# Queries and keys as scaled fp16 pairs that stay on chip, and an FFN in eight blocks

## The chip, the cores and the metric

The kernel runs on one core of one Trainium2 chip. The metric is device microseconds from start to end of one execution. The engines are named as in the profile: PE (TensorE, matmuls), PEld (its weight loads), DVE (VectorE), ACT (ScalarE), POOL (GpSimd), SP (SyncE, which here only issues DMAs). Each engine works through its own instructions strictly in the order in which they were written to it.

## The reference

Clustered attention, then a maxout FFN. There are 4 batches, 8 heads, 768 positions and a head size of 64; queries, keys and 16 centroids per head are normed, each query and key belongs to the centroid with the largest product, and a query sees only keys of its own cluster.

```python
mask = q_assign[:, :, :, None] == k_assign[:, :, None, :]
scores = scale * np.matmul(q, k.transpose(0, 1, 3, 2))
scores = np.where(mask, scores, -1000000000.0)
attn = softmax(scores)
attn_out = np.matmul(attn, v)                     # (4, 8, 768, 64) -> x (3072, 512)
h = np.maximum(np.maximum(x @ w1, x @ w2), x @ w3)  # (3072, 768)
out = h @ w_out                                   # (3072, 512)
```

Inputs and output are fp32.

## The kernel before

To keep fp32's accuracy, every operand of a matmul is held as a pair of a rounded part and the rest, and each product is summed from two or three matmuls. q and k of one head stand in one tile of 128 partitions: q^T in the upper 64, k^T in the lower 64. The tile `qk` of a pair of heads holds four versions of both heads (`AQ, BQ, BK, AK`, two heads, 768 columns), made from the loaded `stage` tile: `qk_prep` casts the high part to fp32r (ACT) and subtracts it for the low part (POOL, once DVE), and `qk_moves` copies parts between the upper and the lower 64 partitions, by DMA from batch 1 on, by ACT and POOL in batch 0. Two matmuls per half row then give the whole score: one of 128 rows (`aq` with `ak`), one of `K2` = 80 rows (`bq` with `bk`), whose last 16 rows carry the one-hot cluster of the query and that of the key, shifted by `BIG`, so that a pair of different clusters gets a large negative score. `cluster_scores` multiplies the pair with the centroids, `cluster_rows` finds the winner by two block transposes and compares on DVE, and writes the one-hot rows into the qk tile.

One **step** is one head and 128 queries (`scores`): four score matmuls into a `big` tile of PSUM (three buffers), a scaled negation with row minimum on DVE (line 489), the exponential on ACT (line 492), the reciprocal of the sum on DVE, and the split of the probabilities into two fp16 halves `hl`, by ACT and DVE (lines 502 and 503) or, in the steps that `by_pool` names, by POOL and ACT (498 to 500). A DMA transpose (line 504) carries `hl` into `pt`. Three steps make a query half of one head; then `av` multiplies with v (12 matmuls of 384 columns, six against 128 weight columns and six against 64), and after both heads of a pair `x_split` (POOL) makes the fp16 pair `x16`, the FFN's input.

There are 192 steps, 48 for a batch. In batch 0 the pairs are visited for query half 0 one after the other (24 steps), and then for half 1 in the order 1, 2, 3, 0; only the qk tiles of two to three pairs fit, so pair 0 of batch 0 is loaded and prepared a second time, with its cluster rows from a copy in DRAM (`AGAIN`, `dpool`, `qk_masks`), and pair 0 of batch 1 has its clusters computed early from another load (`cluster_early`). From batch 1 on each pair is visited for both halves at once.

The FFN works on blocks of 384 tokens, that is one query half of one batch (`ffn_units`): 18 hidden units of 12 matmuls (line 555, 384 columns) with a maximum on DVE (567), and three output units of 18 matmuls of 512 columns (589), an ACT copy (598) and a DMA (600). A block needs all four pairs of its half. The two blocks of batch 0 are spread over steps 30 to 95 (`F_0`), those of batches 1 and 2 over the 48 steps of the next batch, and the two of batch 3 come at the end. Weights are fetched and turned into fp16 pairs during the first 52 steps (`W_A`, `W_B`, `W_O`).

The order of the work comes from a list: `spread` gives each unit a step and a priority (its step plus an offset such as `PREP_LATE` = -9), and the scheduling layer writes the instructions of each engine by priority, as far as buffers and data are there by its own estimate of times. `behind` holds a unit until a named instruction has been issued.

## Time and profile before

| what | value |
|---|---|
| median of 3 runs (lowest, highest) | 876.4 us (874.48, 883.78) |
| span of the profiled execution | 882.8 us |
| its own time: the slowest listed run is the nearest | 883.78 us |
| busy: PE, DVE, ACT, POOL | 722.7, 617.5, 529.3, 498.3 us |
| DMA: bytes, share of 16 engines | 144.38 MB, 79.1% |
| mean granted clock of PE | 0.905 of full speed |
| first exponential, 25th, 49th, last | 23.9, 129.0, 236.9, 762.6 us |

A row of the table of groups reads: line, engine, operation, output and inputs, shapes and count; then the busy time in us and the mean length of one in ns; then the time for which the engine was idle just before them, and what ended that. Matmuls overlap in their records, so the time that one costs is the group's busy time by its count, not its mean length. A row of windows gives the stretch, its length, the busy time of each engine with the number of instructions, the granted clock, the busy share of the 16 DMA engines and GB/s.

### The profile page before, as it was taken

Reading aid. Unit: us, or ns where it says so; the run is one execution under the profiler, and the core shown is the slowest. Engines: PE = TensorE matmul, PEld = TensorE weight load, DVE = VectorE, ACT = ScalarE, POOL = GpSimd, SP = SyncE. Lnnn points to the kernel's source line nnn. Section 1 sums busy time; section 2 is a strip of 40 time slices with the busy share of each in tenths; the row PEclk is TensorE's granted clock in tenths of the full one; section 3 lists DMA queues with packets and bytes.
Section 4 is the critical chain, followed back from the end, with each engine's and each line's share of the span. In section 5 each row is a group of like instructions: output and inputs, shape, how many; then the busy total and the mean of one; then the engine's idle time right before and its main releaser. Section 6 shows DMA issues by size and latency. Waiting matters only on the chain.

```text
span 882.8 us, 12105 instructions
## 1 busy us (share of the span) xinstructions
PE 722.7 (82%) x3836; PEld 425.1 (48%) x3836; DVE 617.5 (70%) x1327; ACT 529.3 (60%) x915; POOL 498.3 (56%) x490
## 2 busy tenths in 40 slices
PE   3534766766777888988898988989988999999997
PEld 2312444443443455644555545655555566556463
DVE  7968878897999757878889866976677677501110
ACT  7655677863866566777676746766667577520101
POOL 4796684673945355767586735676657436412121
PEclk9756565868996998999999999999999999999999
DMA  7863978999988879999998989797898677720000
GB/s 249 218 167 74 201 140 189 227 207 226 238 190 166 187 167 196 177 206 186 213 226 189 232 197 190 144 199 177 169 200 146 122 155 132 136 62 1 36 1 36
DMA packets 330367, 145.14 MB, mean 164 GB/s; under 512 B 304576, under 2 KB 313792, under 8 KB 330304
## 3 DMA queue, kind: packets, MB, share of 16 engines
q1 hardware_dynamic: 330304, 144.38, 79.1%
q8 instruction: 30, 0.49, 0.2%
q14 instruction: 33, 0.27, 0.1%
HBM read 38.57 MB, written 7.08 MB: 52 GB/s over the span
## 4 chain that ended last, share of the span: by engine, by line
PE 26%; DMA 15%; DVE 13%; ACT 7%; issue 6%; POOL 4%; SPq 2%; ACTq 0%; POOLq 0%; DVEq 0%
PE one L555 13%; DMA pt<-hl 12%; PE one L589 6%; DVE big L489 4%; DVE hl L503 4%; ACT hl L502 3%; DMA stage<-in_v_dram 2%; PE one L514 2%; ACT e L492 2%; SPq L504 1%; POOL hl L500 1%; PE big L484 1%; PE one L517 1%; PE big L486 1%; DVE cl_t L441 1%
## 5 line engine op out<-in xcount | busy, mean ns | idle before, releaser
L503 DVE SCALAR_TENSOR_TENSOR hl<-e,r,hl 128x768 f16<-128x768 f32 x147 | 194.9, 1331 | 56.7 <-ACT hl L502 54.6
L555 PE MATMUL one<-x,w16a 128*128 128x384 f16 x1152 | 207.8, 336 | 20.5 <-ACT vf_h L565 4.7
L492 ACT ACTIVATE e<-big,nm 128x768 f32<-128x768 f32 x192 | 172.0, 897 | 81.4 <-DVE big L489 30.1
L489 DVE TENSOR_SCALAR_CACHE_REDUCE big<-big 128x768 f32<-128x768 f32 x192 | 181.6, 960 | 16.2 <-PE big L486 15.7
L502 ACT ACTIVATE hl<-e,r 128x768 f16<-128x768 f32 x147 | 135.9, 931 | 77.0 <-DMA pt<-hl 62.0
L484 PE MATMUL big<-qk 128*128 128x512 f32 (+1 forms) x384 | 127.9, 416 | 54.5 <-ACT e L492 50.6
L555 PEld LDWEIGHTS <-w16a 128*128 128x128 f16 x1152 | 111.3, 100 | 104.4 <-issue 40.3
L486 PE MATMUL big<-qk 80*128 80x512 f32 (+1 forms) x384 | 111.8, 374 | 8.6 <-DMA qk<-cl_t 4.6
L514 PE MATMUL one<-pt,v 128*128 128x384 f16 x384 | 82.5, 356 | 38.0 <-DMA pt<-hl 15.3
L484 PEld LDWEIGHTS big<-qk 128*128 128x128 f32 x384 | 68.9, 211 | 89.2 <-ACT e L492 66.6
L555 PE MATMUL one<-x,w16b 128*128 128x384 f16 x576 | 102.2, 332 | 9.4 <-ACT xt L523 5.0
L500 POOL TENSOR_TENSOR hl<-e,hl 128x768 f16<-128x768 f32 x45 | 78.9, 1759 | 45.4 <-ACT hl L499 44.9
L555 PEld LDWEIGHTS <-w16b 128*128 128x128 f16 x576 | 55.3, 99 | 49.5 <-issue 16.7
L486 PEld LDWEIGHTS big<-qk 80*128 80x128 f32 x384 | 67.4, 212 | 22.4 <-DVE qk L455 4.5
L527 POOL TENSOR_TENSOR xs<-xs,xt 128x384 f32<-128x384 f32 x32 | 35.2, 1101 | 66.1 <-ACT xt L523 63.8
L514 PEld LDWEIGHTS <-v 128*128 128x128 f16 x384 | 37.2, 104 | 70.3 <-issue 41.9
L365 POOL TENSOR_TENSOR qk<-stage,qk 128x768 fp32r<-128x768 f32 x32 | 64.8, 2042 | 8.3 <-ACT qk L362 8.1
L499 ACT CAST hl<-e 128x768 f16<-128x768 f32 x45 | 37.2, 829 | 42.4 <-DMA pt<-hl 30.0
L567 DVE SCALAR_TENSOR_TENSOR wf_h<-one,wf_h 128x384 f32<-128x384 f32 x48 | 26.5, 552 | 49.9 <-PE one L555 44.9
L498 POOL TENSOR_SCALAR e<-e,r 128x768 f32<-128x768 f32 x45 | 43.7, 975 | 28.0 <-DVE r L494 21.0
L567 DVE SCALAR_TENSOR_TENSOR vf_h<-one,vf_h 128x384 f32<-128x384 f32 x48 | 26.3, 549 | 46.3 <-PE one L555 46.3
L573 POOL TENSOR_SCALAR wf_h<-wf_h 128x384 f16<-128x384 f32 x24 | 15.5, 646 | 74.6 <-DVE wf_h L567 70.6
(133 smaller groups left out, 1061.3 us busy)
## 6 DMA issues: line engine op xcount, KB each, us to landing
stage<-in_qk_dram SPq DMA_DIRECT2D x36, 384.0 KB, 4.6
qk<-qk SPq DMA_DIRECT2D x28, 384.0 KB, 4.6
stage<-in_v_dram SPq DMA_DIRECT2D x25, 384.0 KB, 4.4
wd<-in_moe_w_dram SPq DMA_DIRECT2D x18, 512.0 KB, 5.3
qk<-qk SPq DMA_DIRECT2D x12, 768.0 KB, 6.5
out_dram<-o SPq DMA_DIRECT2D x24, 256.0 KB, 2.5
pt<-hl SPq DMA_TRANSPOSE x192, 4.3
wd<-in_moe_w_out_dram SPq DMA_DIRECT2D x6, 512.0 KB, 5.2
```

The source lines that it names most:

```text
L365: last["lo"] = eng.tensor_tensor(t[:, AQ, i], x, t[:, BQ, i].bitcast(F32), op=ALU.subtract)
L484: nc.tensor.matmul(t[:, lo:hi], aq[:, qs], ak[:, lo:hi], start=True, stop=False)
L486: last["pe"] = nc.tensor.matmul(t[:, lo:hi], bq[0:K2, qs], bk[0:K2, lo:hi], start=False, stop=True)
L489: last["nm"] = nc.vector.tensor_scalar(e, e, -SCALE, 3.0e38, op0=ALU.mult, op1=ALU.min, accum_out=nm)
L492: nc.scalar.activation(x, e, AF.Exp, bias=nm, scale=-1.0, accum_out=r)
L500: nc.gpsimd.tensor_tensor(hl[:, 1, :], x, hl[:, 0, :], op=ALU.subtract)
L502: nc.scalar.activation(hl[:, 0, :], x, AF.Copy, scale=r)
L503: nc.vector.scalar_tensor_tensor(hl[:, 1, :], x, r, hl[:, 0, :], op0=ALU.mult, op1=ALU.subtract)
L514: nc.tensor.matmul(t[:, 0:NB], vt, pt[:, :, kt, :], start=(kt == 0), stop=False)
L555: nc.tensor.matmul(t[:, 0:NB], w16[jt // JA][:, jt % JA, wa, i, ct], x16[b, gi, ct][:, xa, :], start=(n == 0), stop=(n == 3 * CT - 1),)
L567: nc.vector.scalar_tensor_tensor(m, t[:, 0:NB], 2.0**-24, ms[jt], op0=ALU.mult, op1=ALU.max)
L589: nc.tensor.matmul(t[:, 0:DM], h16[jt][:, ha, tt * P : (tt + 1) * P], wo16[0][:, jt, wa, :], start=(n == 0), stop=(n == 3 * JT - 1),)
```

## The change

q and k become fp16 pairs. Because fp16's range is small, a power of two for q and one for k of each pair of heads is found first (`qk_scale`: an absolute maximum per partition on DVE, over both heads; a matmul with the identity that lays the 128 maxima out along a row; a maximum over each 64 of them; the reciprocals), the split multiplies by it (`qk_split`: in batch 0's pair 0 by ACT and DVE, elsewhere a scaling by POOL, a cast by ACT, a difference by POOL), and the negation of the scores undoes it with the factor `nsc`. `BIG` becomes 61440, which is in fp16's range, with a second one-hot copy (`onehot2`), so that `K2` is 96 rows. The centroids' weights become fp16.

A qk tile is half as large, and there are four of them: each pair is loaded once, `AGAIN`, the DRAM tile and `cluster_early` go. Every batch now visits all four pairs for half 0 and then all four for half 1. Each half has its own FFN block in the half that follows (24 steps), and one block remains at the end. In batch 0 the copies between the halves of the qk tile are made by DVE. The next batch's pair is prepared as soon as its predecessor in half 1 is done (`prep_units` from step t+1 to t+10). The weights are due a few steps earlier, staging has four buffers for three, `x16` eight for ten, and `by_pool` names 53 steps for 45.

```diff
-BIG = 2.0**100
+BIG = 61440.0
+CSC = 2.0**10
...
-        return sb.tile([P, S], F32, tag="stage", name="stage", bufs=3)
+        return sb.tile([P, S], F32, tag="stage", name="stage", bufs=4)
...
-    def qk_prep(b, pr, i, pool, again=False):
-        x = load(b, 2 * pr + i)
-        if i == 0:
-            qkt[b, pr] = pool.tile([P, 4, 2, S], F32R, tag="qk", name="qk", bufs=2 if pool is sb else 1)
-        t = qkt[b, pr]
-        last["hi"] = nc.scalar.copy(t[:, BQ, i], x)
-        xin[i] = x
-        eng = nc.vector if (b, pr) < (1, 1) and QK_LO[b * NPAIR + pr + (b == 0 and again) * (NPAIR + 1)] else nc.gpsimd
-        last["lo"] = eng.tensor_tensor(t[:, AQ, i], x, t[:, BQ, i].bitcast(F32), op=ALU.subtract)
+    def qk_load(b, pr):
+        xin[b, pr] = xs = []
+        for i in range(2):
+            x = stage()
+            nc.sync.dma_start(out=x, in_=qk[b, 2 * pr + i])
+            xs.append(x)
+
+    def qk_scale(b, pr):
+        m2 = sb.tile([P, 2], F32, tag="q_m2", name="q_m2", bufs=2)
+        for i, x in enumerate(xin[b, pr]):
+            nc.vector.tensor_reduce(m2[:, i : i + 1], x, axis=AX.X, op=ALU.max, apply_absolute_value=True)
+        m = sb.tile([P, 1], F32, tag="q_m", name="q_m", bufs=2)
+        nc.vector.tensor_scalar(m, m2[:, 0:1], m2[:, 1:2], 2.0**-10, op0=ALU.max, op1=ALU.max)
+        nc.vector.tensor_scalar(m.bitcast(I32), m.bitcast(I32), 0x7F800000, None, op0=ALU.bitwise_and)
+        a = one()[:, 0:P]
+        nc.tensor.matmul(a, m.bitcast(BF16)[:, 1:2].broadcast_to([P, P]), ident16, start=True, stop=True)
+        p2 = sb.tile([P, 2], F32, tag="q_p", name="q_p", bufs=2)
+        nc.vector.tensor_reduce(p2, a.rearrange("p (g d) -> p g d", g=2), axis=AX.X, op=ALU.max)
+        r2 = sb.tile([P, 2], F32, tag="q_r", name="q_r", bufs=2)
+        nc.vector.reciprocal(r2, p2)
+        nc.vector.tensor_tensor(r2, r2, hsel, op=ALU.mult)
+        s = sb.tile([P, 1], F32, tag="q_s", name="q_s", bufs=2)
+        nc.vector.tensor_reduce(s, r2, axis=AX.X, op=ALU.add)
+        n = nsc[b, pr] = cpool.tile([P, 1], F32, name=f"nsc_{b}_{pr}")
+        nc.vector.scalar_tensor_tensor(n, p2[:, 0:1], -SCALE, p2[:, 1:2], op0=ALU.mult, op1=ALU.mult)
+        qsc[b, pr] = s
+
+    def qk_split(b, pr):
+        s = qsc[b, pr]
+        t = qkt[b, pr] = sb.tile([P, 4, 2, S], F16, tag="qk", name="qk", bufs=QK_BUFS)
+        for i, x in enumerate(xin.pop((b, pr))):
+            if (b, pr) < (1, 0) and QK_LO[pr]:
+                last["hi"] = nc.scalar.activation(t[:, BQ, i], x, AF.Copy, scale=s)
+                last["lo"] = nc.vector.scalar_tensor_tensor(
+                    t[:, AQ, i], x, s, t[:, BQ, i], op0=ALU.mult, op1=ALU.subtract
+                )
+            else:
+                nc.gpsimd.tensor_scalar(x, x, s, 1.0, op0=ALU.mult, op1=ALU.mult)
+                last["hi"] = nc.scalar.copy(t[:, BQ, i], x)
+                last["lo"] = nc.gpsimd.tensor_tensor(t[:, AQ, i], x, t[:, BQ, i], op=ALU.subtract)
...
-            nc.scalar.copy(t[up, AK], x[dn, BQ])
-            nc.scalar.copy(t[up, BK], x[dn, BQ])
...
+        nc.vector.tensor_copy(t[up, AK], t[dn, BQ])
+        nc.vector.tensor_copy(t[up, BK], t[dn, BQ])
+        if pr:
+            nc.sync.dma_start(out=t[dn, AK], in_=t[dn, AQ])
         else:
-            nc.gpsimd.tensor_scalar(t[dn, AQ], x[up, BQ], 1.0, 1.0, op0=ALU.mult, op1=ALU.mult)
+            nc.vector.tensor_copy(t[dn, AK], t[dn, AQ])
+        nc.vector.tensor_copy(t[dn, AQ], t[up, BQ])
...
         nc.vector.tensor_scalar(
-            onehot[D:P, :, 0:C], onehot[D:P, :, 0:C], 1.0, BIG, op0=ALU.subtract, op1=ALU.mult
+            onehot2,
+            onehot.rearrange("p n (r c) -> p n r c", r=1).broadcast_to([P, n, 2, C]),
+            ksel,
+            BIG,
+            op0=ALU.subtract,
+            op1=ALU.mult,
         )
...
-    K2 = D + C
+    K2 = D + 2 * C
...
-        last["nm"] = nc.vector.tensor_scalar(e, e, -SCALE, 3.0e38, op0=ALU.mult, op1=ALU.min, accum_out=nm)
+        last["nm"] = nc.vector.tensor_scalar(e, e, nsc[b, h // 2], 3.0e38, op0=ALU.mult, op1=ALU.min, accum_out=nm)
...
+    QK_BUFS = 4
...
-    W_A, W_B, W_O = (4, 33), (30, 43), (38, 52)
-    F_0 = ((30, 52), (56, 59)), ((54, 85), (86, 95))
+    W_A, W_B, W_O = (3, 26), (24, 36), (32, 46)
...
+                t = at + HS + V * (pr + 1)
+                spread(prep_units(b + 1, pr), t + 1, t + 10, PREP_LATE)
+        for gi in range(NG):
+            k = HS * (NG * b + gi + 1)
+            if (b, gi) < (B - 1, NG - 1):
+                h, o = ffn_units(b, gi)
+                spread([u for j in h for u in j], k + 3, k + HS, F_LATE)
+                spread(o, k + HS, k + HS + 3, F_LATE)
+    visits = [(b, pr, gi) for b in range(B) for gi in range(NG) for pr in range(NPAIR)]
```

Where instructions come to stand: first DVE, from the centroids to the first cluster transpose of pair 0 of batch 0, before (`c` is the scaled centroids, `qk` the pair's tile, `vf` the staged v):

```order
L151 TENSOR_SCALAR c_133<-c_sb,c_yr 128x128
L365 TENSOR_TENSOR qk<-stage,qk 128x768
L166 TENSOR_TENSOR cw<-one,cw 64x4x16 x4
L365 TENSOR_TENSOR qk<-stage,qk 128x768
L312 TENSOR_REDUCE vmax<-vf 128x1
L429 STREAM_TRANSPOSE cl_t<-big 128x768
```

and the same place now (`q_p`, `q_r`, `q_s` and `nsc` belong to the scale of q and k):

```order
L376 TENSOR_REDUCE q_p<-one 128x2
L378 RECIPROCAL q_r<-q_p 128x2
L383 SCALAR_TENSOR_TENSOR nsc_0_164<-q_p 128x1
L170 SCALAR_TENSOR_TENSOR cw<-one,cw 64x4x16 x4
L379 TENSOR_TENSOR q_r<-q_r,hsel 128x2
L381 TENSOR_REDUCE q_s<-q_r 128x1
L392 SCALAR_TENSOR_TENSOR qk<-stage,q_s,qk 128x768 x2
L408 COPY qk<-qk 64x1536
L409 COPY qk<-qk 64x1536
L316 TENSOR_REDUCE vmax<-vf 128x1
L413 COPY qk<-qk 64x1536
L432 STREAM_TRANSPOSE cl_t<-big 128x768
```

The end of the scale and three copies have come in ahead of the transpose; the fourth stands behind it.

Next ACT in batch 1, from the exponential of the 83rd step on (`e<-big`), before. `wf_h` is a hidden unit of the FFN, `xs` and `xt` the result of an `av`, `qk<-stage` the cast of the next pair:

```order
L492 ACTIVATE e_3342,r_3341<-big_3334,nm_3339 128x768
L362 CAST qk_3508<-stage_3506 128x768
L362 CAST qk_3508<-stage_3511 128x768
L502 ACTIVATE hl_3316<-e_3312,r_3311 128x768
L492 ACTIVATE e_3376,r_3375<-big_3368,nm_3373 128x768
L565 ACTIVATE wf_h_2312<-one_3251 128x384
L502 ACTIVATE hl_3346<-e_3342,r_3341 128x768
L492 ACTIVATE e_3411,r_3410<-big_3403,nm_3408 128x768
```

and now the rows up to the exponential of the 84th step:

```order
L517 ACTIVATE xs_3274<-one_3489 64x384
L518 ACTIVATE xt_3275<-one_3489 64x384
L497 ACTIVATE hl_3708<-e_3704,r_3703 128x768
L560 ACTIVATE vf_h_3456<-one_3556 128x384
L517 ACTIVATE xs_3274<-one_3604 64x384
L518 ACTIVATE xt_3275<-one_3604 64x384
L397 CAST qk_3689<-stage_3586 128x768
L397 CAST qk_3689<-stage_3588 128x768
L560 ACTIVATE vf_h_3456<-one_3721 128x384
L517 ACTIVATE xs_3537<-one_3735 64x384
L518 ACTIVATE xt_3538<-one_3735 64x384
L487 ACTIVATE e_3758,r_3757<-big_3750,nm_3755 128x768
```

Three attention products, the casts of pair 0 of batch 2 and two hidden units now stand between two exponentials, where at most two rows and a pair of casts stood. On PE the 84th score stands behind the first cluster matmul of that pair, and between the 83rd and the 84th score are 102 FFN matmuls and three products with v. The same pattern returns ahead of the 132nd score, and in batch 0 ahead of the 36th (78 FFN matmuls behind the 35th) and the 42nd (72).

Last SP, the end of the program before (`pt<-hl` are the transposes, `out_dram<-o` the output blocks):

```order
L504 DMA_TRANSPOSE pt<-hl 128x12x128 x3
L600 DMA out_dram<-o 128x512
L457 DMA qk<-cl_t 16x768 x4
L600 DMA out_dram<-o 128x512 x2
L504 DMA_TRANSPOSE pt<-hl 128x12x128 x24
L600 DMA out_dram<-o 128x512 x9
```

and now:

```order
L460 DMA qk<-cl_r 32x768 x4
L499 DMA_TRANSPOSE pt<-hl 128x12x128 x17
L595 DMA out_dram<-o 128x512 x2
L499 DMA_TRANSPOSE pt<-hl 128x12x128 x3
L595 DMA out_dram<-o 128x512
L499 DMA_TRANSPOSE pt<-hl 128x12x128 x18
L595 DMA out_dram<-o 128x512 x6
```

Behind the last transpose nine output blocks have become six.

More of the change, by code (lines that the diff above doesn't have):

```diff
@@ L653, in at_prio @@
         u(*args)
[L655 to L659 removed]
+    c_sb = load_centroids()
+    first = prep_units(0, 0)
     vm = v_max_first()
[L661 removed]
     first[0]()
     centroids(c_sb)
[L664 to L668 removed]
+    for u in first[1:5]:
+        u()
     behind("lo", vm[0])
[L670 removed]
+    first[5]()
     wa = [u for j in range(JA) for u in w_units(fp[0], j)]
```

190 lines of the change are left out of this document (61 added, 129 removed).

## The prediction

> **What bounds the kernel now.** I read the slices of the page first, to see how many different stages the span has.
>
> ```profile
> PE   3534766766777888988898988989988999999997
> DVE  7968878897999757878889866976677677501110
> POOL 4796684673945355767586735676657436412121
> PEclk9756565868996998999999999999999999999999
> DMA  7863978999988879999998989797898677720000
> ```
>
> No engine is full from end to end. On the left DVE and the DMA engines are high and PE is low, with its granted clock cut in many slices; in the middle PE and DMA are at 8 and 9; in the last five slices only PE works. So the span has to be priced by stages, and I cut it at the starts of the exponentials (ACT, line 492, one per attention step of 128 queries): the first 24 steps are query half 0 of batch 0, the next 24 are half 1, then come 144 steps of batches 1 to 3.
>
> ```profile
> L492 ACT ACTIVATE e<-big,nm x24: 880/901/903, 23.9 to 125.5; 128x768 f32<-128x768 f32 x24
> L492 ACT ACTIVATE e<-big,nm x24: 880/894/902, 129.0 to 235.5; 128x768 f32<-128x768 f32 x24
> L492 ACT ACTIVATE e<-big,nm x144: 881/901/905, 236.9 to 762.6; 128x768 f32<-128x768 f32 x144
> ```
>
> The table of windows at these borders has the busy time of each engine, the granted clock and the DMA share in each stage.
>
> ```profile
> core 0: us, PE busy (x) PEld busy (x) DVE busy (x) ACT busy (x) POOL busy (x), PEclk, DMA share, GB/s
> 0.00:23.90 23.90, 9.53 (x23) 6.17 (x24) 17.45 (x31) 16.92 (x25) 12.61 (x33) 1.00 0.74 243
> 23.90:129.00 105.10, 55.01 (x196) 33.15 (x195) 88.31 (x177) 67.59 (x114) 79.12 (x73) 0.62 0.74 159
> 129.00:236.90 107.90, 75.98 (x338) 43.50 (x338) 88.15 (x193) 74.00 (x127) 68.61 (x71) 0.78 1.01 216
> 236.90:762.60 525.70, 467.52 (x2629) 279.65 (x2628) 406.78 (x898) 352.93 (x620) 314.66 (x284) 0.96 0.91 181
> 762.60:882.80 120.20, 114.61 (x654) 62.64 (x653) 16.85 (x31) 17.91 (x33) 23.32 (x32) 1.00 0.14 37
> ```
>
> Batch 0 (23.9 to 236.9) is led by DVE: 176.5 of 213.0 us, 83%, with the DMA engines full in its second half and PE far from it. Batches 1 to 3 are led by PE, 467.5 of 525.7 (89%), with DMA right behind it at 0.91. The last 120.2 us are the FFN of batch 3, both query halves, on PE alone. What waits end last in the middle stage, the waits of that window tell:
>
> ```profile
> ACT hl L502 <- DMA pt<-hl: 54.9, 33, 5.5
> DVE hl L503 <- ACT hl L502: 47.1, 44, 4.7
> ```
>
> The probabilities wait for the DMA transposes to free their buffers: there PE is not the only limit. I sum against this execution, whose span is 882.8; the slowest listed run, 883.78, stands 0.98 above that, and I take it for its own time. It is 0.84% above the median of the runs, 876.4, so the result is scaled by 876.4/883.8.
>
> **The change part by part: the tail.** One of the two FFN blocks at the end moves into the attention. Its price stands in the tail:
>
> ```profile
> L555 PE MATMUL one<-x,w16a 128*128 128x384 f16 x288 | 47.1, 326 | 0.0
> L555 PE MATMUL one<-x,w16b 128*128 128x384 f16 x144 | 23.7, 326 | 0.0
> L589 PE MATMUL one<-wo,vf_h 128*128 128x512 f16 x54 | 12.0, 379 | 0.8 <-ACT o L598 0.8
> L589 PE MATMUL one<-wo,wf_h 128*128 128x512 f16 x54 | 12.0, 379 | 0.8 <-ACT o L598 0.8
> ```
>
> That is 94.8 us for two blocks, 47.4 for one. By the order of the built programs 420 FFN matmuls stand behind the last score instead of 654: 234 fewer, 180 of 0.164 us and 54 of 0.222, which is 41.5 us. The last block then starts as soon as its own x is split, where the block of the other half covered that before. Bounds 0 and 5 us; I take 2.5. Tail: **-39**.
>
> **The start and batch 0.** The preparation of q and k now begins with a scale: two absolute maxima over 128x768, a small matmul, seven tiny DVE operations, and only then the split. In batch 0 the copies between the halves of the qk tile move from ACT and POOL to DVE.
>
> ```profile
> L293 DVE TENSOR_REDUCE vmax<-stage 128x1 f32<-128x768 f32 x12 | 11.4, 949 | 9.9 <-DMA stage<-in_v_dram 9.6
> L279 DVE TENSOR_SCALAR wo<-wo,r_o 128x1024 f16<-128x1024 f16 x6 | 2.5, 478 | 0.0
> L375 ACT CAST qk<-qk 64x1536 fp32r<-64x1536 f32 x4 | 5.9, 1471 | 0.1
> L100 DVE TENSOR_SCALAR sc_m<-sc_m 128x1 f32<-128x1 f32 x11 | 1.5, 143 | 0.0
> ```
>
> In front of the first score stand the two maxima (1.9), the tiny ones (seven of 0.14 to 0.3, about 1.2), and four copies, less what ACT did there: I take **+6**, bounds +2 and +10. Over the first 48 steps the order puts on DVE: 16 maxima of 0.949 (15.2); about 55 tiny ones of 0.15 (8); 13 copies of 64x1536 fp16. No row shows such a copy: the fp16 row of line 279 bounds it below at 0.48, the ACT copy above at 1.47; by elements, 1.5 times line 279 gives 0.72, hence 9.4. Then work that used to lie later: one more chain of cluster rows (about 6), the last weight conversions (12), five FFN maxima (2.7), less the old splits and two probability splits (-4). Together about 50 us on an engine that had 36.5 idle in 213.0. How full can DVE be? Two windows later it was at 22.00 and 21.52 of 22:
>
> ```profile
> 242.00:264.00 22.00, 16.98 (x102) 10.38 (x100) 22.00 (x46) 13.81 (x25) 11.43 (x13) 1.00 0.90 190
> 264.00:286.00 22.00, 14.65 (x60) 8.31 (x61) 21.52 (x57) 14.95 (x27) 13.02 (x11) 0.69 0.77 169
> ```
>
> At 94%, between that and its 83%, (176.5+50)/0.94 = 241 us: **+28**. Bounds: +13 if it runs at all but full, +50 if its idle time stays. ACT is relieved by about 10 us there and costs nothing. The FFN block that runs in these steps lies on PE, which had 82 us free.
>
> **Batches 1 to 3.** PE: the order has 1536 FFN matmuls between the 48th and the last score for 1398, 138 x 0.18 = +25. The scores become fp16. What a back-to-back fp32r set costs at full clock, the trace shows:
>
> ```profile
> 486.32 0.64 PE L484 MATMUL big<-qk 128*128 128x512 f32 x2
> 486.80 0.51 PE L486 MATMUL big<-qk 80*128 80x512 f32 x2
> 487.15 1.15 PE L514 MATMUL one<-pt,v 128*128 128x384 f16 x6
> ```
>
> From 486.32 to 487.15 are 0.83 us for 1536 columns. The FFN rows above give 0.164 us per 384 columns of fp16 and 0.222 per 512, so 0.66 for the same set. That saves 0.17 a step, 24 in 144 steps (bounds 0 and 40), and some 4 in the cluster scores. PE's need stays where it was, 467. DMA falls:
>
> ```profile
> q1 hardware_dynamic: 330304, 144.38, 79.1%
> stage<-in_qk_dram SPq DMA_DIRECT2D x36, 384.0 KB, 4.6
> qk<-qk SPq DMA_DIRECT2D x28, 384.0 KB, 4.6
> qk<-qk SPq DMA_DIRECT2D x12, 768.0 KB, 6.5
> ```
>
> The moves inside SBUF were 28 x 384 + 12 x 768 KB; at two bytes an element, with three moves in batch 0 instead of four and the rest in DVE, half is left: 10 MB fewer, 3 more for four loads and the mask's round trip, 9% of 144.38. Over this stage that takes the share from 0.91 to about 0.84, and with it some of the 54.9 us. DVE's rows stay even: 11 scale chains of 3.1 come, weight conversions and probability splits go. I take **-14**, a quarter of that wait; bounds -35 (PE at 95%) and +25 (fp16 no faster, or SP held up: a pair's two loads now wait for staging buffers that are free only when POOL and ACT have split the pair before, and the next transposes are queued behind them on SP).
>
> Sum: -39 +6 +28 -14 = -19: a span of 864, own time 865, scaled **858**. Its own range, half of each distance to a bound added up in squares (-12, +22), is 846 to 880.
>
> **The rivals.** *The middle follows PE more closely (faster):* with DMA at 0.84 the stage runs at 95% PE, -31 instead of -14, and DVE in batch 0 at 99%, +15: 835 in its own time, 828. For it: in the stretch behind 300 the DMA digits are 9 and the wait for transposes is the largest. Against it: DVE's share does not fall.
>
> *The burst (slower):* in the new order the cluster matmuls of the next batch's pair 0 stand ahead of the 84th score (and the 132nd) on PE, as the order shows, and ahead of them 102 FFN matmuls and three products with v: 84 x 0.164 + 18 x 0.222 = 17.8, and three times the 1.15 of the row above for six matmuls with as many narrower ones behind, about 5; 23 us. The cluster matmul waits for ACT's cast, that for POOL's scaling, that for the small matmul behind the burst; every later score is queued behind it. ACT and DVE have about 5 us of steps buffered (three score tiles) and 8 of preparation; then some 12 to 15 us of attention work is lost, which later steps must make up at DVE's pace. Twice, and once more for the two smaller bursts in batch 0: +40. It decides if the buffers run dry while PE is in the burst. 905 in its own time, 897. For it: the rows of the order; against it: PE works through the burst.
>
> *DVE's idle time stays (same):* +50 instead of +28 gives 880. *The port that DVE and POOL share:* in the trace a DVE operation with two SBUF inputs stretches while POOL works.
>
> ```profile
> L503 DVE SCALAR_TENSOR_TENSOR hl<-e,r,hl x147: 969/1020/8622, 31.6 to 766.3; 128x768 f16<-128x768 f32 x147
> 57.80 8.62 DVE L503 SCALAR_TENSOR_TENSOR hl<-e,r,hl 128x768 f16<-128x768 f32 x1
> L503 DVE SCALAR_TENSOR_TENSOR hl<-e,r,hl 128x768 f16<-128x768 f32 x35 | 53.8, 1542 | 6.8 <-ACT hl L502 6.7
> L196 DVE SCALAR_TENSOR_TENSOR wf<-wd,top 128x512 int32<-128x512 int32 x21 | 21.9, 1045 | 4.7 <-ACT top L194 4.6
> L498 POOL TENSOR_SCALAR e<-e,r 128x768 f32<-128x768 f32 x45 | 43.7, 975 | 28.0 <-DVE r L494 21.0
> ```
>
> In batch 0 line 503 took 1.542 at the mean against a median of 1.020, 18 us over 35; line 196 adds about 7. POOL gets 30 scalings of 0.975 (10 to 12 of them in batch 0) and eight more probability splits. If the stretching grows in step with POOL and reaches the new copies and the wider one-hot, 20 us come on top: 885 in its own time, 878. The Trainium skill ("SBUF — State Buffer", section "Who interferes with whom") says that a DVE copy or tensor_scalar in a two-port mode, and any DVE operation with two SBUF inputs, fully blocks against a POOL operation: by it the added fp16 copies would both block and be blocked, which is this rival; the 8.62 us row agrees for two inputs, and for copies no row here shows it. *fp16 no faster than fp32r, the change not doing what it says:* +24 in the middle, 882.
>
> **How the numbers follow.** Forecast 0.42, closer to PE 0.18, burst 0.20, idle DVE 0.08, port 0.07, fp16 0.05. "Faster" (over 1%, about what a measurement of this kernel can tell from no change: under 867.6) takes the fast rival and four fifths of the forecast: 0.52. "Same" takes the last fifth and the three that end near 880, less their far ends: 0.25. "Slower" (over 885.2) is the burst and those far ends: 0.23. The range runs from just below the fast rival, 822, to the burst, 897.
>
> **What would show it.** The profile after should have its first exponential near 30, the 49th near 270, the last 48 to 50 us of PE alone behind the last attention product; a DMA total near 132 MB; DVE at 94% in batch 0; a score set near 0.66. It is wrong if the exponentials of batches 1 to 3 span over 540 us (burst) or batch 0 over 260 (DVE, port).

## The result, and the profile after

The changed kernel takes **911.2 us** (median of 4 runs, 907.48 to 914.7) beside 875.6 for the kernel before in the same job: a ratio of **1.040, 95% interval [1.034, 1.045]**, slower. Forecast were 858, with a range of 822 to 897. The profiled execution has a span of 908.1 us, 25.3 more than before; that of before is the slowest of its four runs (883.78 us, median 875.6), so the spans differ by 25.3 us only where the medians differ by 35.6, and a span below 882.8 is not yet a faster kernel.

The slices of the page after, to be held against those of before: DVE is as high as before on the left, DMA is lower nearly everywhere (131.01 MB for 144.38), and the stretch of PE alone at the right end is shorter.

```profile
PE   1042556567748789999688979989788999989997
DVE  7869896867999698954687798836586889565010
DMA  6328578875976889668669967766778778587200
q1 hardware_dynamic: 330144, 131.01, 68.4%
```

The windows at the starts of the exponentials (line 487 now) divide the span as the prediction did. Batch 0 is cut once more here, at the first step of pair 1 (step 6; steps are counted from 0) and at half 1 (step 24). First after, then the rows of before that the prediction did not cut so (its third row, 129.0 to 236.9, is steps 24 to 47).

```profile
core 0: us, PE busy (x) PEld busy (x) DVE busy (x) ACT busy (x) POOL busy (x), PEclk, DMA share, GB/s
25.90:93.10 67.20, 19.99 (x78) 8.23 (x78) 54.95 (x111) 25.57 (x43) 41.09 (x40) 0.87 0.49 123
93.10:156.10 63.00, 35.14 (x130) 13.92 (x129) 50.78 (x113) 43.30 (x74) 50.23 (x46) 0.64 0.77 164
156.10:289.30 133.20, 89.40 (x450) 43.95 (x449) 113.93 (x269) 77.10 (x134) 90.98 (x95) 0.81 0.77 169
289.30:830.00 540.70, 479.84 (x2764) 254.57 (x2764) 399.33 (x926) 349.20 (x613) 312.53 (x296) 0.96 0.76 152
...
830.00:908.10 78.10, 73.54 (x420) 39.75 (x419) 11.40 (x21) 13.44 (x24) 16.16 (x22) 0.99 0.19 47
```
```profile
23.90:68.00 44.10, 16.46 (x54) 9.90 (x53) 36.76 (x62) 26.81 (x43) 35.33 (x32) 0.60 0.74 188
68.00:129.10 61.10, 38.54 (x142) 23.25 (x142) 51.55 (x116) 40.88 (x73) 43.88 (x41) 0.64 0.74 138
```

| stage | before | after | difference | forecast |
|---|---|---|---|---|
| to the first exponential | 23.9 | 25.9 | +2.0 | +6 |
| batch 0, steps 0 to 5 (pair 0) | 44.1 | 67.2 | +23.1 | |
| batch 0, steps 6 to 23 | 61.1 | 63.0 | +1.9 | |
| batch 0, steps 24 to 47 | 107.8 | 133.2 | +25.4 | |
| batch 0 together | 213.0 | 263.4 | **+50.4** | +28 |
| batches 1 to 3 | 525.7 | 540.7 | **+15.0** | -14 |
| behind the last exponential | 120.2 | 78.1 | -42.1 | -39 |
| sum | 882.8 | 908.1 | +25.3 | -19 |

The loss has two places inside batch 0, each with a pause. The first stands right behind the first exponential. In the order of time on PE, with the idle time before a row and what ended it in brackets:

```profile
40.88 0.31 PE L374 MATMUL one<-ident,q_m 128*128 128x128 bf16 x1
...
51.40 0.58 PE L424 MATMUL big<-qk,cw 128*128 128x512 f16 x1 [9.67 <-ACT qk L397]
51.77 0.84 PE L479 MATMUL big<-qk 128*128 128x512 f16 x2
```
```profile
35.03 3.98 POOL L338 TENSOR_SCALAR vf<-vf,s_v 128x768 f32<-128x768 f32 x4 [31.13 <-DMA wd<-in_moe_w_dram]
40.02 7.58 POOL L343 TENSOR_TENSOR v<-vf,v 128x384 f16<-128x384 f32 x8 [1.01 <-ACT v L342]
47.58 2.02 POOL L209 TENSOR_SCALAR wf<-wf,s_w 128x512 f32<-128x512 f32 x3
49.58 3.54 POOL L396 TENSOR_SCALAR stage<-stage,q_s 128x768 f32<-128x768 f32 x4
```

The second score (line 479, 51.77) is queued on PE behind the scale products of pairs 1 and 2 (line 374) and the first cluster matmul of pair 1 (424). That one waits for ACT's cast, the cast for POOL's scaling (396), and the scaling stands on POOL behind 13.6 us of v and weights (lines 338, 343, 209), which began only at 35.03. The second exponential starts 30.2 us after the first.

The second place is step 35. Pair 3 had its maxima (line 369) long before; then PE does this:

```profile
L369 DVE TENSOR_REDUCE q_m<-stage x2: 942/948/953, 106.1 to 112.2; 128x1 f32<-128x768 f32 x2
```
```profile
203.47 2.11 PE L550 MATMUL one<-x,w16a 128*128 128x384 f16 x12 [1.24 <-DVE sc_m L103]
...
209.04 0.22 PE L374 MATMUL one<-ident,q_m 128*128 128x128 bf16 x1 [0.95 <-DVE w_s L266]
209.10 4.06 PE L550 MATMUL one<-x,w16a 128*128 128x384 f16 x24
213.21 1.14 PE L509 MATMUL one<-pt,v 128*128 128x384 f16 x6
214.27 0.68 PE L512 MATMUL one<-pt,v 128*64 128x384 f16 x6
214.88 2.12 PE L550 MATMUL one<-x,w16a 128*128 128x384 f16 x12
216.84 0.38 PE L424 MATMUL big<-qk,cw 128*128 128x512 f16 x1
217.06 0.49 PE L479 MATMUL big<-qk 128*128 128x512 f16 x2
```

The scale's product comes 96 us after its maxima, behind FFN matmuls and products with v; then more of these, the first cluster matmul, and only then the score. Between two exponentials lie 29.6 us here, 18.1 at step 41, 20.6 at step 47, and in batches 1 to 3 19.9 at step 83 and 22.9 at step 131. Why the product came so late, the places of the tiles suggest: its output is a `one()` tile, from a PSUM ring of two buffers in which FFN and the products with v take theirs, and the cluster product takes a `big()` tile ahead of the next scores. If a ring is handed out in the order in which the program asks, the product cannot pass the FFN units that asked earlier, and the score cannot pass the cluster product. That was the theory to test (the **ring link**), against the load of DVE, the late release of the qk tile, and, later, the chain of pair 1.

### The profile page after: what moved, and what is told of

The parts are those of the page before. It is cut to its first block, busy times and chain, and to the rows that moved or that the text cites. A ratio compares the mean times of both kernels' runs of the same rounds, so it can differ in the third digit from the quotient of the medians.

```text
span 908.1 us, 12205 instructions
## 1 busy us (share of the span) xinstructions
PE 703.0 (77%) x3852; PEld 362.0 (40%) x3852; DVE 649.6 (72%) x1478; ACT 515.0 (57%) x897; POOL 514.2 (57%) x527
## 3 DMA queue, kind: packets, MB, share of 16 engines
q1 hardware_dynamic: 330144, 131.01, 68.4%
## 5 line engine op out<-in xcount | busy, mean ns | idle before, releaser
L484 DVE TENSOR_SCALAR_CACHE_REDUCE big<-big,nsc 128x768 f32<-128x768 f32 x192 | 192.6, 1015 | 52.3 <-PE big L481 52.0
L498 DVE SCALAR_TENSOR_TENSOR hl<-e,r,hl 128x768 f16<-128x768 f32 x139 | 167.1, 1210 | 37.7 <-ACT hl L497 36.5
L497 ACT ACTIVATE hl<-e,r 128x768 f16<-128x768 f32 x139 | 126.5, 929 | 52.7 <-DMA pt<-hl 28.6
L479 PE MATMUL big<-qk 128*128 128x512 f16 (+1 forms) x384 | 104.1, 354 | 56.6 <-ACT e L487 42.5
L550 PE MATMUL one<-x,w16b 128*128 128x384 f16 x576 | 106.3, 333 | 5.6 <-ACT xt L518 2.8
L481 PE MATMUL big<-qk 96*128 96x512 f16 (+1 forms) x384 | 103.6, 351 | 5.3 <-DVE qk L462 5.3
L479 PEld LDWEIGHTS <-qk 128*128 128x128 f16 x384 | 36.7, 102 | 120.8 <-issue 89.8
L493 POOL TENSOR_SCALAR e<-e,r 128x768 f32<-128x768 f32 x53 | 54.2, 1024 | 32.5 <-DVE r L489 27.4
L584 PE MATMUL one<-wo,vf_h 128*128 128x512 f16 x216 | 55.0, 411 | 10.2 <-DVE q_p L376 3.7
L517 ACT ACTIVATE xs<-one 64x384 f32<-64x384 f32 x64 | 30.7, 480 | 52.5 <-PE one L512 47.6
L398 POOL TENSOR_TENSOR qk<-stage,qk 128x768 f16<-128x768 f32 x30 | 53.8, 1808 | 1.4 <-ACT qk L397 1.3
```

The source lines that it names most:

```text
L398: last["lo"] = nc.gpsimd.tensor_tensor(t[:, AQ, i], x, t[:, BQ, i], op=ALU.subtract)
L479: nc.tensor.matmul(t[:, lo:hi], aq[:, qs], ak[:, lo:hi], start=True, stop=False)
L481: last["pe"] = nc.tensor.matmul(t[:, lo:hi], bq[0:K2, qs], bk[0:K2, lo:hi], start=False, stop=True)
L484: last["nm"] = nc.vector.tensor_scalar(e, e, nsc[b, h // 2], 3.0e38, op0=ALU.mult, op1=ALU.min, accum_out=nm)
L493: nc.gpsimd.tensor_scalar(x, x, r, 1.0, op0=ALU.mult, op1=ALU.mult)
L497: nc.scalar.activation(hl[:, 0, :], x, AF.Copy, scale=r)
```

## The experiments

Spans and windows below are those of each run's profiled execution, times are medians, ratios are against the kernel before on the same chip, with their 95% interval in brackets. Which kernel is faster, the ratios say and not the spans. Stages of all runs, in us:

| kernel | first exp | steps 0-5 | 6-23 | 24-47 | batches 1-3 | span |
|---|---|---|---|---|---|---|
| before | 23.9 | 44.1 | 61.1 | 107.8 | 525.7 | 882.8 |
| changed | 25.9 | 67.2 | 63.0 | 133.2 | 540.7 | 908.1 |
| e1 no scale | 29.6 | 42.3 | 73.3 | 108.5 | 534.2 | 866.9 |
| e2 link only | 23.5 | 60.1 | 60.6 | 124.4 | 535.8 | 882.6 |
| e3 scale in big | 24.8 | 66.9 | 62.9 | 107.6 | 544.1 | 884.4 |
| e4 scale earlier | 26.2 | 66.2 | 72.9 | 123.2 | 544.5 | 911.3 |
| e5 out two terms | 25.8 | 67.0 | 62.9 | 133.3 | 521.8 | 882.0 |
| e6 before, two terms | 23.9 | 43.5 | 60.3 | 106.5 | 514.2 | 856.9 |
| e7 half transposes | 26.1 | 73.1 | 64.4 | 137.2 | 517.9 | 899.6 |
| e8 big, copies on ACT | 24.5 | 58.4 | 71.0 | 116.0 | 543.0 | 891.1 |
| e9 split ACT and DVE | 24.6 | 63.1 | 61.4 | 115.0 | 547.5 | 890.1 |
| e10 rows on DVE | 24.6 | 52.6 | 80.9 | 106.3 | 549.0 | 891.7 |
| e11 both, small | 24.7 | 58.2 | 65.3 | 115.9 | 544.5 | 886.7 |
| e12 squares on ACT | 27.2 | 70.1 | 61.9 | 121.0 | 538.5 | 897.0 |
| e13 pair 1 earlier | 32.2 | 31.7 | 80.4 | 121.4 | 533.1 | 877.0 |
| e14 pair 1 not held | 32.3 | 40.7 | 79.4 | 115.8 | 544.1 | 890.7 |
| e15 big, no maxima | 22.2 | 55.8 | 63.1 | 112.4 | 538.7 | 870.4 |
| e16 pair 1, squares | 31.4 | 31.7 | 78.4 | 115.3 | 537.1 | 872.4 |
| e17 the same, copies | 31.3 | 31.5 | 79.1 | 111.4 | 540.4 | 871.8 |

**The ring link and the work of the scale, e1 to e4.** e1 puts a constant in the scale's place:

```diff
-        m2 = ...; maxima; matmul; p2, r2, s, n as in qk_scale
+        s, nsc[b, pr] = const        # 2**12, -SCALE * 2**-24
```


> Leaves out: the scale of every q/k pair (both maxima, the product on PE that spreads them, the small DVE operations); a fixed power of two stands in for it. All else as in the changed kernel. Theory A (ring): the product of qk_scale takes a tile of the two-buffer PSUM ring that it shares with the FFN and the products with v, so it goes to PE only behind 100 FFN matmuls; the cluster product waits for it, and the scores that take their tile of the big ring behind the cluster product wait for that. Without qk_scale both links are gone: the pauses of 20 to 30 us between exponentials at steps 35, 83 and 131 disappear, batches 1 to 3 take 490 to 515 us instead of 540.7, the span is 840 to 870. Theory B (DVE work): 16 pairs x 2 maxima x 0.95 = 30 us and some 16 x 1.4 = 22 us of small operations leave DVE, in batch 0 on the path: batch 0 is 10 to 15 us shorter, the rest unchanged, span 885 to 900. Theory C (the fp16 pair's buffer is free only after its last score, so the cluster product is late whatever feeds it): the pauses stay, span over 895.

e2 keeps the product, its ring and what hangs on it, without the maxima:

```diff
-        nc.vector.tensor_reduce(m2[:, i : i + 1], x, ...)   # twice, then two operations
+        m = const[0]                                        # 1.0
         a = one()[:, 0:P]
```


> Leaves out: the two maxima of every q/k pair and the two DVE operations on them; a constant 1 goes through the same product on PE, the same five small DVE operations and the same scaling. So the DVE work is 30 us less, but the place of the product in the two-buffer ring is kept. Theory A: the pauses at steps 35, 83 and 131 stay at 18 to 30 us, span 885 to 905 (a few us from DVE in batch 0). Theory B: most of the gain of the kernel without the scale is here too, its span within 10 us of that one. Theory C: as A.

e3 keeps all the work and takes only the link away:

```diff
-        a = one()[:, 0:P]
+        cl[b, pr] = big()
+        a = cl[b, pr][:, S : S + P]
```


> Computes all that the changed kernel does. Only the PSUM tile of the product in qk_scale changes: the unused columns 768 to 895 of the tile that the cluster product of the same pair takes anyway (ring of three), instead of a tile of the ring that FFN and the products with v use. Theory A: the pauses at steps 35, 83 and 131 go, batches 1 to 3 at 490 to 520 us, span 845 to 880 (batch 0 keeps its DVE work). Theory B and C: no change, 900 to 915. Against it: the tile of the big ring is held some us longer, from the product to the transpose, which leaves two for scores.

e4 moves the request for the tile ahead in the program, in batches 1 to 3:

```diff
-                spread(prep_units(b + 1, pr), t + 1, t + 10, PREP_LATE)
+                spread(u[:2], t - 10, t - 8, PREP_LATE)      # load, scale
+                spread(u[2:], t + 4, t + 10, PREP_LATE)
```


> Computes all that the changed kernel does. For batches 1 to 3 the loads and the scale of a pair stand 10 to 11 steps earlier in the program (so does the place in the two-buffer ring), split, cluster product, moves and rows where they stood; batch 0 is unchanged. Theory A: the pauses at steps 83 and 131 go, those of batch 0 (35, 41, 47) stay; batches 1 to 3 at 490 to 520 us, span 865 to 890. Theory B and C: no change, 900 to 915.

Measured: e1 has 869.2 us (ratio 0.993 [0.988, 0.998]), e2 884.1 (1.013 [1.005, 1.021]), e3 885.1 (1.013 [1.002, 1.023]), e4 910.9 (1.042 [1.033, 1.051]). The link is real: the built order on PE between steps 80 and 83, with the number of matmuls (F: FFN, AV: with v, QS: scale product, PS: that of v, CL: cluster, S: score), changes with the ring alone.

```
changed: S80 .. PS F18 AV12 S82 F42 AV12 F36 AV12 QS F24 AV12 CL1 S83
e3:      S80 F11 QS F6 PS F19 AV12 S81 CL1 S82 CL2 F17 CL5 F13 S83
```

In e3 no pause of over 12 us is left behind step 43, and steps 24 to 47 take 107.6 as in the kernel before (107.8). Its second exponential comes 9.9 us after the first instead of 30.2, but 32.9 us now lie ahead of step 6, the first of pair 1, so that steps 0 to 5 stay at 66.9. The windows of e3 (batch 0 in three parts, then batches 1 to 3) and of e1 (batches 1 to 3):

```profile
24.80:91.70 66.90, 23.11 (x73) 8.98 (x74) 61.79 (x115) 26.57 (x46) 50.82 (x45) 0.91 0.55 138
91.70:154.60 62.90, 36.42 (x143) 14.35 (x140) 56.64 (x119) 41.55 (x73) 39.19 (x38) 0.66 0.69 151
154.60:262.10 107.50, 75.61 (x350) 35.87 (x349) 100.41 (x227) 73.32 (x125) 90.57 (x91) 0.76 0.82 191
262.10:806.30 544.20, 496.89 (x2857) 264.13 (x2857) 420.48 (x955) 352.90 (x621) 317.55 (x303) 0.97 0.77 154
```
```profile
253.80:788.00 534.20, 487.85 (x2850) 261.47 (x2849) 401.40 (x887) 352.98 (x621) 316.00 (x300) 0.97 0.78 155
```

But Theory A had its gain in the wrong stage. It gave 490 to 520 us for batches 1 to 3 in e1, e3 and e4, and they stay at 534 to 545 in all three; the 24 us of e3 come from batch 0. e4 shows it by itself: the pauses at steps 83 and 131 are gone (11.8 us at most from step 59 on), and it is no faster (910.9 us for 911.2). From step 60 to 168 the changed kernel takes 413.8 us, e4 403.2, e3 408.3; e2 takes 415.1 there and e15 (below), which differs from it by the ring alone, 398.6. These 6 to 17 us are not the price of the pauses alone, because the kernels without the pauses have more FFN matmuls left for batches 1 to 3. Theory C fell with e3. Theory B holds its part: the maxima and the two operations on them are worth 20.7 us of start and batch 0 (e2: 268.6 for 289.3), the link 27.2 (e3: 262.1), both together 35.5 (e1: 253.8) or 35.8 (e15, which differs from e3 by the maxima and those two operations alone: 253.5). The two overlap: with the other already gone, the link is worth 15.1 and the maxima 8.6. So e2 is nearer to e1 than the ring theory gave it (885 to 905) and farther than the DVE theory did.

**What bounds batches 1 to 3, e5 to e7.** e5 and e6 leave PE work out of the changed kernel and of the one before, e7 DMA work.

```diff
-                    for ha, wa in HLS:          # output product
+                    for ha, wa in HLS[:2]:      # e5, e6
```
```diff
-        ... dma_start_transpose(out=pt[:, g], in_=hl.rearrange("p a s -> p (a s)"))
+        ... dma_start_transpose(out=pt[:, g], in_=hl[:, 0, :])      # e7
```


> The changed kernel; leaves out the third of the three terms in FFN's output product (h low by wo high), 18 of 270 FFN matmuls of a block, on PE alone: 108 fewer in batches 1 to 3, by the rows of the changed kernel (79.8 us for 324) 26.6 us less PE there, and 4 us in the tail. Theory P (batches 1 to 3 go by PE at 89% busy, whatever the order): 540.7 falls by 25 to 30, span 872 to 882. Theory T (they go by the chain scores, DVE, ACT, transpose, with the pauses as loss): by less than 10, span 895 to 905. Theory D (DMA transposes are the bound): unchanged but the tail, 900 to 906.

> The kernel before, with the same term left out: 90 fewer matmuls in batches 1 to 3 (62.2 us for 270), 20.7 us less PE, and 8 us in the tail. Theory P: 525.7 falls by 19 to 23, span 850 to 856. Theory T and D (the waits for the DMA transposes, 54.9 us of ACT's, set the pace): by less than 10, span 865 to 875.

> The changed kernel; leaves out the transposes of the low parts of the probabilities (half of the transposed data; a tile of zeros stands in the second product with v), so that PE, ACT, DVE and POOL keep all their instructions and DMA loses some 40% of its bytes. Theory P: batches 1 to 3 stay within 10 us of 540.7, batch 0 too, span 895 to 910. Theory D: batches 1 to 3 fall by 30 or more. Theory T: by 10 to 30, since a transpose lands sooner and frees its buffer.

Batches 1 to 3 of e5, e6 and e7, in this order:

```profile
289.10:810.90 521.80, 461.95 (x2655) 244.30 (x2655) 393.48 (x925) 348.82 (x613) 310.99 (x296) 0.95 0.78 157
```
```profile
234.20:748.40 514.20, 453.23 (x2541) 271.87 (x2540) 400.67 (x898) 353.58 (x621) 313.82 (x284) 0.96 0.95 185
```
```profile
300.90:818.80 517.90, 472.34 (x2760) 252.33 (x2761) 398.32 (x927) 348.80 (x612) 307.33 (x295) 0.97 0.49 105
```

The medians are 886.1, 859.1 and 899.8 us. e5: 17.9 us less PE, 18.9 us less time; e6: 14.3 less PE, 11.5 less time, between the theories. The 26.6 and 20.7 us that I gave for the term were too much: the busy times of single lines add up to more than PE's busy time, and PE lost only 17.9 and 14.3. Measured by PE's own loss, the changed kernel follows PE one for one and the one before by eight tenths, at shares of 0.88 to 0.89. e7 speaks against Theory P alone: with half of the transposed data the share rises to 0.912 and 22.8 us go, 7.5 of them with PE's own time, while the waits of ACT and PE for the transposes fall from 25.8 and 24.2 us to 7.2 and 15.7. Its batch 0 is 11.4 us longer, where Theory P had no change; I have no cause for that. The share of 0.89 is thus PE with the wait for transposes in it, and the two are not cleanly apart.

**Batch 0 without the link, e8 to e12.** All five are e3 with work moved between DVE, ACT and POOL. e8: copies of pairs 1 to 3 to ACT (`cp = nc.scalar.copy if pr else nc.vector.tensor_copy`) and smaller tiny operations. e9: `QK_LO = (1, 1, 1, 1)`. e10: `ROWS = (1, 1, 1, 0, 0)`. e11: both, with e8's tiny operations. e12:

```diff
-            nc.vector.tensor_reduce(m2[:, i : i + 1], x, ..., op=ALU.max, apply_absolute_value=True)
+            nc.scalar.activation(junk, x, AF.Square, accum_out=m2[:, i : i + 1])
```


> Computes all that the changed kernel does. As the kernel with the scale's product in the big ring, and in batch 0 three of the four 64x1536 copies of pairs 1 to 3 go to ACT (nine copies, 10.7 us of DVE in that run), the factor is formed by two reciprocals on half the partitions instead of reciprocal, multiply and sum, and nsc by an operation with one tensor input (these two-input tiny ones took 10.9 us). Theory: batch 0 goes by DVE once the ring link is gone (219 of 237.4 us, 92%); 20 us less DVE gives 215 to 222 for it, batches 1 to 3 stay at 535 to 545, span 862 to 872, which is the time before within 2%. Rival (the copies' latency on ACT and POOL, not DVE's load, sets batch 0): 232 to 240, span 880 to 890.

> Computes all that the changed kernel does: the kernel with the scale's product in the big ring, and in batch 0 all four pairs are scaled and split by ACT and DVE (as pair 0 is) instead of POOL, ACT, POOL: some 5 us of POOL less and 2 to 4 us of DVE more for each of pairs 1 to 3. Theory Q (the first twelve steps, 85.5 us in that kernel against 67.7 without the scale, are set by the chain that prepares pair 1, in which POOL operations wait behind POOL's other work): they fall to 72 to 80, span 870 to 880. Theory V (DVE is full there, 80.0 of 85.5 us, so DVE's load sets them): they rise by 3 to 8, span 886 to 895.

> Computes all that the changed kernel does: the kernel with the scale's product in the big ring, and the two 128x384 operations in the cluster rows of pairs 1 and 2 of batch 0 go from POOL to DVE. In that kernel the first of them waited 13 us on POOL behind v and the weights, and the rows of pair 1 took 38 us from the cluster product to the mask. Theory Q: the first twelve steps fall from 85.5 to 70 to 78, span 868 to 878. Theory V: four more operations of 0.5 to 1.0 us on a full DVE, 86 to 90 for the first twelve steps, span 884 to 890.

> Computes all that the changed kernel does: both edits of the last two, with the factor formed by two reciprocals on half the partitions and nsc by an operation with one tensor input. Theory Q: the first twelve steps at 66 to 74, batch 0 at 215 to 225, span 860 to 872. Theory V: as the two before added up, 88 to 96, span 885 to 900.

> Computes all that the changed kernel does, with another power of two as scale: as the kernel with the scale's product in the big ring, and the 32 maxima of DVE (14 of 0.94 us = 13.2 us in batch 0) become 32 sums of squares on ACT (about 0.9 us each), from which the power of two is formed (one tiny DVE operation more). Theory V (batch 0 goes by DVE, 92% busy, once the ring link is gone): 13.2/0.92 = 14 us less there, 237.4 falls to 221 to 227; batches 1 to 3 stay within 8 of 544; span 866 to 876. Rival W (batch 0 is set by the chain of the preparation, whose length stays, not by DVE's load, as moving copies to ACT suggested): 234 to 245, span 880 to 892.

Measured: e8 889.4 (1.014 [1.008, 1.020]), e9 890.8, e10 893.4, e11 888.8 (1.013 [1.005, 1.020]), e12 899.2 (1.027 [1.024, 1.030]); e3 had 885.1. None gained. e8, e10 and e11 shorten steps 0 to 5 (58.4, 52.6 and 58.2 for 66.9) and lose it behind. e12 takes 12.2 us of maxima from DVE in batch 0, and DVE's busy time there stays at 217 us (e3: 219), because other operations stretch (the widening of the one-hot rows from 5.8 to 9.6 us, five operations in both) and two tiny ones for each pair are new; its squares wait on ACT for their loads, 9.3 us of that within the pause ahead of step 6, which grows from 32.9 to 40.1 us. Neither "DVE's load" nor "the chain" alone explains these five.

**Pair 1's chain and DVE's load together, e13 to e17.** e13 is e3 with pair 1 prepared ahead of the first score; e14 only does not hold its load and scale behind line 484; e15 is e3 with e2's constant; e16 is e13 with squares on ACT from pair 3 on; e17 is e16 with six copies on ACT and one tiny operation changed.

```diff
+    u1 = prep_units(0, 1)
+    u1[0]()                                  # load, ahead of pair 0's scale
     for u in first[1:5]:
         u()
     ...
+    u1[1]()                                  # scale
-    spread([... behind("nm", u) for u in prep_units(0, 1)], 0, 1, -10)
+    spread([... behind("nm", u) for u in u1[2:]], 0, 1, -10)
```


> Computes all that the changed kernel does: the kernel with the scale's product in the big ring, and pair 1 of batch 0 is loaded and scaled with pair 0, ahead of the first score, its split, cluster product, moves and rows as early as the order lets them. No work is added or taken away. Theory X (the first twelve steps are set by the chain that prepares pair 1, load to mask, which the scale lengthens): the first exponential comes 3 to 10 us later, the first of pair 1 follows it after 40 to 52 us instead of 66.9, start and batch 0 together (262.1) fall by 8 to 20, span 865 to 877. Theory V (DVE's load sets them): start and batch 0 together stay within 5 us of 262.1, span 880 to 890.

> Computes all that the changed kernel does: the kernel with the scale's product in the big ring, and only the load and scale of pair 1 of batch 0 are no longer held behind the first score's DVE operation (line 484). Theory X: as the kernel with pair 1 earlier, half of its gain, span 873 to 880. Theory V: 880 to 890.

> The kernel with the scale's product in the big ring; leaves out the two maxima of every pair and two tiny operations on them, a constant 1 goes through the product and the scaling. Theory V: 13 us of DVE less in batch 0, which falls from 237 to 222 to 226, as without the scale (224). Theory X: the maxima are 2 us of pair 1's chain, and the chain waits little less: the first exponential of pair 1 after 58 to 66 us, batch 0 at 229 to 237.

> Computes all that the changed kernel does, with another power of two as scale: the kernel with pair 1 earlier and the scale's product in the big ring, and from pair 3 of batch 0 on the maxima of DVE become sums of squares on ACT (10 of 0.94 us in batch 0). Theory V (with the ring link and pair 1's late chain gone batch 0 goes by DVE at 94%): start and batch 0 together fall from 265.7 by 8 to 11 to 255 to 258, batches 1 to 3 at 530 to 540, span 862 to 872. Rival W (something else, such as ACT's order, sets it): 262 to 272, span 873 to 885.

> Computes all that the changed kernel does, with another power of two as scale: as the last one, and three of the four 64x1536 copies of pairs 2 and 3 of batch 0 go to ACT (six of about 1.2 us), and nsc is formed with one tensor input. Theory V: 7 to 9 us less than the last one, start and batch 0 together at 246 to 250, span 855 to 865. Rival W: no gain over the last one, or some us worse (the kernel with nine copies on ACT was 8 us longer in batch 0).

Measured: e13 882.0 (1.003 [1.0005, 1.006]), e14 889.8, e15 875.2 (0.995 [0.992, 0.998]), e16 **875.3 (0.996 [0.993, 0.999])**, e17 877.5 (0.998 [0.995, 1.002]). The windows of e13 (steps 0 to 5, 6 to 23, 24 to 47) and of e16 (24 to 47):

```profile
32.20:63.90 31.70, 12.67 (x36) 4.68 (x36) 31.45 (x68) 18.71 (x32) 18.31 (x16) 1.00 0.57 139
63.90:144.30 80.40, 39.60 (x157) 15.72 (x157) 72.93 (x137) 47.24 (x85) 66.85 (x65) 0.75 0.74 163
144.30:265.70 121.40, 78.09 (x386) 38.64 (x384) 114.75 (x245) 73.64 (x129) 88.16 (x89) 0.80 0.78 175
```
```profile
141.50:256.90 115.40, 75.28 (x388) 38.19 (x387) 110.93 (x242) 77.68 (x138) 89.28 (x90) 0.82 0.81 182
```

e13 halves steps 0 to 5, as Theory X said, and gives all of it back: start and batch 0 together are 265.7 for 262.1, as Theory V said (its span is shorter by 7.4, its median by 3.2, since batches 1 to 3 have 13 us less PE, which I did not expect of it). DVE is then at 219.1 of 233.4 us, 94%. In that state DVE's load is the price: e16 takes 9.4 us of maxima away and start and batch 0 fall by 8.8, to 256.9, inside the 255 to 258 that was expected. e17 takes more, but its DVE is at 192 of 222 us only (86%), so that another limit, which I did not find, begins there; it gains 3.7 of the 7 to 9 in batch 0 and nothing in the whole. e14 gained nothing, as Theory V said, and e15 missed Theory V: its batch 0 is 231.3, where V had 222 to 226, with DVE at 87%. So with DVE near 87% its load is no longer the whole limit. e16 is a version with the reference's computation that is level with the kernel before, 0.4% ahead by its ratio, no more.

## Why the prediction was wrong, point by point

**Tail, -39: right** (-42.1). PE has 420 matmuls behind the last exponential for 654, 36 of them with v in both kernels: 234 FFN matmuls fewer, as the order had it.

**Start, +6: +2.0**, at the bound.

**fp16 scores, 0.66 a set: right.** From 398.21 to the next row are 0.67 us for four matmuls:

```profile
398.21 0.50 PE L479 MATMUL big<-qk 128*128 128x512 f16 x2
398.55 0.49 PE L481 MATMUL big<-qk 96*128 96x512 f16 x2
398.88 1.46 PE L584 MATMUL one<-wo,wf_h 128*128 128x512 f16 x6
```

**Batch 0, +28: +50.4, the first step that failed.** The work was sized well: DVE has 219.7 us there for 176.5, +43, where I gave about 50. What failed is "how full can DVE be?": I took 94%, and DVE stayed at 83%. The bound of +50 that I had named and weighed with 0.08 is met partly by luck: it was made of 50 us of new work and idle time that stays, measured are 43.2 of work and 7.2 more idle time. What keeps DVE from filling is a new wait of the change, the ring link. Without it (e3) DVE has the same busy time in start and batch 0 (238.1 us for 238.9), the stretch is 27.2 us shorter, and DVE is at 92% of batch 0. Of the 25.7 us by which steps 24 to 47 fall in e3, 12.2 are idle time of DVE and 13.5 are DVE work that the changed kernel does there and e3 elsewhere (113.93 and 100.41 in the windows). The other place of the loss, steps 0 to 5 (+23.1, with 18.2 more DVE work), has the chain of pair 1 behind the first score, to which the scale adds two maxima, a product and seven tiny operations, and which is worked off behind v and the weights on POOL. That this chain costs time by itself is not shown: with it moved ahead as well (e13) DVE is at the 94% that I had taken and the stage is 233.4, +20.4 against the forecast of +28, but the start is 32.2, +8.3 against +6, and the two together are 3.6 us longer than in e3.

**Batches 1 to 3, -14: +15.0, the second step that failed.** It had two halves. "PE's need stays where it was, 467": it is 479.8, and e5 shows that this is paid one for one. Between the 49th and the last exponential lie 163 more FFN matmuls (1561 for 1398, after and before below), where the order has 138 more between the scores.

```profile
L550 PE MATMUL one<-x,w16a 128*128 128x384 f16 x864 | 151.2, 327 | 6.8 <-ACT o L593 3.7 <-ACT xt L518 2.4 <-DVE q_p L376 0.8
L550 PE MATMUL one<-x,w16b 128*128 128x384 f16 x373 | 70.2, 331 | 5.2 <-ACT xt L518 2.8 <-DVE r L488 1.2 <-ACT wf_h L560 0.9
L584 PE MATMUL one<-wo,vf_h 128*128 128x512 f16 x162 | 43.0, 421 | 10.2 <-DVE q_p L376 3.7 <-DVE r L488 3.6 <-ACT xt L518 2.9
L584 PE MATMUL one<-wo,wf_h 128*128 128x512 f16 x162 | 36.8, 379 | 1.5 <-ACT o L593 1.3
```
```profile
L555 PE MATMUL one<-x,w16a 128*128 128x384 f16 x720 | 130.0, 333 | 9.7 <-DVE wf_h L567 3.8 <-ACT wf_h L565 2.5 <-ACT vf_h L565 1.9
L555 PE MATMUL one<-x,w16b 128*128 128x384 f16 x408 | 74.4, 334 | 8.5 <-ACT xt L523 4.2 <-ACT vf_h L565 3.2 <-DVE r L493 0.8
L589 PE MATMUL one<-wo,vf_h 128*128 128x512 f16 x162 | 36.4, 380 | 0.0
L589 PE MATMUL one<-wo,wf_h 128*128 128x512 f16 x108 | 25.8, 389 | 1.6 <-DVE wf_h L567 1.6
```

At the prices of the prediction (0.18 a matmul, -0.17 a score set, -4 for the clusters) that makes +1 and not +12. Part of the other 11 us is the price of the scores: if each moment of PE's busy time is counted for the matmul that started first, they take 97.9 us for 112.2, 14 less where I had 24 (in e5 and e6 98.0 for 117.3, 19 less), so that the saving in the stage is 0.10 to 0.14 a set and not the 0.17 that single sets, back to back, gave. The rest stays open. The other half, that less DMA raises PE's share: DMA fell further than forecast (0.91 to 0.76, where I gave 0.84) and the share stayed at 0.887 (479.8 of 540.7). The wait of which I took a quarter even fell, from 54.9 to 25.8 us, and in e3 it is 96.0 (changed, then e3):

```profile
ACT hl L497 <- DMA pt<-hl: 25.8, 15, 3.0
```
```profile
ACT hl L497 <- DMA pt<-hl: 96.0, 57, 5.0
```

So the size of this wait does not tell what the stage can gain. e7 shows that fewer transposes can raise the share (0.912 with half of their data), and e3 has 0.913, the share on which my 511.7 us rested (467/511.7), once no score waits for an FFN block: what held the share down was the ring link (e2 and e15, which also differ by it, have 0.897 and 0.906). At 0.913 the 479.8 us of the changed kernel would take 525.5, at 0.906 instead of 0.897 the 480.7 us of e2 would take 530.7 instead of 535.8; both are estimates. Yet e3 gains nothing in the stage, because its PE need is 496.9: batch 0 has 566 matmuls there instead of 658 (the counts of the windows above added up), since the FFN that the pauses had pulled forward is now done later.

**The burst** was the rival with the right mechanism and the wrong price. The pauses stand where it put them (steps 35, 41, 83, 131), behind the chain that it named. It priced the two in batches 1 to 3 at 12 to 15 us each, and those of batch 0 together at as much as one of them. In batch 0, where DVE has the work and PE time to spare, the link lengthens steps 24 to 47, with three pauses, by 25.7 us. In batches 1 to 3 the price is some 5 to 15 us for both by the estimates above, and it does not show in the stage's time (540.7 with the pauses, 544.2 without), since PE works through the pauses of batch 0 and thereby takes 17 us of FFN out of the later stage (496.9 to 479.8). My counterargument, "PE works through the burst", holds so far; what it overlooked is that DVE and the next scores do not. I also did not see that one PSUM ring forced the order: I read the order and not the tiles that made it so.

**The port** rival was priced as an addition to a full DVE. What the runs show of it stands below; it cannot be told from the rest by any of them alone. Its largest row did not grow: the low halves of the probabilities took 1.269 us at the mean in batch 0, for 1.542 before.

**Two sums** of the prediction are slightly off: a PE busy to 95% would give -34, where it has -31 for the rival and -35 for the bound, and the lower half of its own range comes to -13 instead of -12. Neither moves the forecast.

## What to carry to other kernels

A small product that stands on a critical chain should not take its tile from the ring of a bulk consumer: the ring hands tiles out in the program's order, and the small product then waits for the whole backlog, and all that is queued behind its reader waits too. Price a pause by the engine that bounds its stage: where that engine works through it, the work is done ahead and part of the time comes back later; where it starves, the stage grows. And a share such as "94% busy" is a forecast of its own; ask which new wait could keep the engine from it before the work is divided by it.
